# A second level of the seven-product form inside two of seven products, in an attention and MoE kernel that TensorE bounds

## The chip, the cores and the metric

One core of one Trainium2 chip. The metric is the device time of one execution in microseconds (us), as the median over executions of the same kernel; lower is better. TensorE (PE in the profile) multiplies; VectorE (DVE), ScalarE (ACT) and GpSimd (POOL) do the rest; SyncE (SP) only issues transfers here.

## The reference, cut to what matters

```python
# q, k, v: (8 batches, 8 heads, 576, 64) fp32; w_in (512, 2048); w_out (2048, 512); alpha (2048)
k_p = k.reshape(B, H, 72, 8, D).mean(axis=3)       # keys and values pooled by 8: 72 of them
v_p = v.reshape(B, H, 72, 8, D).mean(axis=3)
attn = softmax(q @ k_p.T / sqrt(D))                # (the sum gets + 1e-9)
x = (attn @ v_p) ...  -> (4608 tokens, 512)
h = x @ w_in                                       # the first MoE product
s = sin(alpha * h)
g = h + s * s / (alpha + 1e-9)
return g @ w_out                                   # the second MoE product
```

## The kernel before

The 4608 tokens are cut into nine **units** of 512. A unit computes the first MoE product in four **groups**; a group is a 2x2 block product by the seven-product form (seven products where the plain form has eight), each product being 2 x 2 matmuls of 128x128 by 256 columns. So a unit has 28 **slots**, seven to a group. Into these slots the kernel puts, by hand, the attention of the batch that the next unit needs: scores, exps, normalisations, "turns" (32x32 transposes on VectorE), "moves" (twelve transfers from SBUF to SBUF that finish the transposition), and at the end the products with the values, which make the next unit's x. Sums of x and of the weights are made on VectorE.

The kernel uses eight PSUM banks. Five belong to the groups, three to the attention:

```python
    def bank(self, shape, i=None):
        if i is None:
            i = self.turn = (self.turn + 1) % 5           # five banks, in turn
        return self.ps_m.tile(shape, F32, name=f"bank{i}")
...
                self.ps_a = pool(att, "ps_a", 3, space=PSUM)
```

In a group the products follow one another in the order 1, 5, 6, 2, 7, 3, 4. Products 6 and 7 accumulate onto a *copy* of an earlier result, which ScalarE makes from one bank into another; the work on a finished product is put into the slot after it:

```python
            def left0(G=G, Q=before):                 # after product 1
                G.b6 = bank()
                nc.scalar.copy(out=G.b6[:], in_=G.b1[:])
                if Q and not early(Q):
                    squares(Q)
            def left1(G=G, Q=before):                 # after product 5
                if Q:
                    self.finish(Q)
            def left2(G=G, Q=before):                 # after product 6
                ...
                G.b7 = bank()
                nc.scalar.copy(out=G.b7[:], in_=G.b6[:])
                G.p5 = self.tp.tile([P, JW, TH], F32, name="p5")
                nc.scalar.copy(out=G.p5[:], in_=G.b5[:])
            ...                                       # left3 to left6: sines, squares, adds
            self.left = [(left0, left1, left2, left3, left4, left5, left6)[k]]
            if k == 1:
                G.b5 = bank()
            p = (1, 5, 6, 2, 7, 3, 4)[k]
            product(p, getattr(G, {1: "b1", 5: "b5", 6: "b6", 2: "b1", 7: "b7", 3: "b6", 4: "b7"}[p]), k < 2)
```

The slots of the attention in units 1 to 6:

```python
            for i in range(5):
                at((1, 3, 4, 5, 6)[i], A.score, i)
                at(8 + (i + 1) // 2, A.exp, i)
                at(9 + (i + 1) // 2, A.norm, i)
                at((12, 12, 13, 14, 14)[i], A.turn, i)
            at(14, A.new_a)
            at(14, A.move, 0)
            at(15, A.move, 1)
            for hp in range(4):
                at((0, 1, 3, 4)[hp], self.load_kv, "v", b, hp)
                ...
                at(24, A.values, hp)
            at(24, A.values_rest)
            turn = 21                                 # turns of the next q but one: slots 21 to 24
```

## Time and profile before

| | before |
|---|---|
| median time | 958.75 us (958.41 to 959.10) |
| span of the profiled run | 956.4 us, mean granted clock 1.000 |
| busy: PE, DVE, ACT, POOL | 98%, 71%, 43%, 21% of the span |
| one unit of 2 to 6 | 57.20 us, no wait of TensorE in it |

The lines behind this stand in the prediction below. How to read them: the busy shares say only which engine to look at first; the chain of waits says what the end of the run hangs on; the table of stretches says whether a repeated part (here the unit) is one engine's work end to end. The last is the strongest here: a unit of 57.20 us that holds 57.20 us of TensorE work cannot be shortened by anything but less TensorE work, and is lengthened by any wait.

### The profile page before, as it was taken

To read this page: it belongs to the slowest core of one execution; us is meant where nothing else is said; L and a number is where in the kernel's file an instruction comes from. 1 tells how busy PE (TensorE), PEld (TensorE's weight loads), DVE (VectorE), ACT (ScalarE), POOL (GpSimd) and SP (SyncE) were. 2 spreads that over 40 slices of the span, in tenths; PEclk is the share of its full clock that TensorE was granted. 3 is DMA by queue.
4 is the path that set the end of the run, shared out by engine and by line. 5 is a ranking of instruction groups with operands and counts; after the bars stand their busy time and mean duration, and the time that the engine had idled before them with its cause. 6 is when DMAs were issued, how large, how long until landed. Compare 5 with 4: busy or idle time off the path is not lost.

```text
span 956.4 us, 18152 instructions
## 1 busy us (share of the span) xinstructions
PE 937.6 (98%) x7259; PEld 833.4 (87%) x7259; DVE 676.5 (71%) x1070; ACT 414.2 (43%) x919; POOL 197.7 (21%) x215
## 2 busy tenths in 40 slices
PE   7998999999999999999999999999999999999998
PEld 3677687887878878787888899999999999999998
DVE  5889585766838577483576996867768695958684
ACT  5376466575756747566555531111111111111111
POOL 1717364443724436260000000000000000000000
PEclk9999999999999999999999999999999999999999
DMA  9636466666576663745615235324142434343201
GB/s 222 176 104 198 125 195 142 205 149 196 171 198 201 156 190 102 188 136 161 242 54 206 98 142 190 125 102 161 67 155 78 143 115 147 98 139 122 100 34 35
DMA packets 84038, 137.88 MB, mean 144 GB/s; under 512 B 10177, under 2 KB 49873, under 8 KB 79345
## 3 DMA queue, kind: packets, MB, share of 16 engines
q1 hardware_dynamic: 83920, 136.70, 47.1%
q8 instruction: 58, 0.95, 0.4%
q14 instruction: 26, 0.21, 0.1%
q10 hardware_dynamic: 34, 0.02, 0.0%
HBM read 74.47 MB, written 47.19 MB: 127 GB/s over the span
## 4 chain that ended last, share of the span: by engine, by line
PE 92%; DVE 4%; ACT 2%; DMA 1%; issue 0%; SPq 0%; DVEq 0%; ACTq 0%
PE bank L489 42%; PE bank L752 30%; PE ps_y L752 12%; PE ps_o L309 3%; PE ps_sc L208 2%; DMA q<-in_q_dram 1%; DVE as L368 1%; ACT s L495 1%; PE ps_at L267 1%; DVE home L462 1%; DVE a L372 1%; PE ps_qt L189 1%; PE bank L452 1%; DVE h L468 0%; PE ps_or L318 0%
## 5 line engine op out<-in xcount | busy, mean ns | idle before, releaser
L489 PE MATMUL bank<-home,a 128*128 128x256 f32 x1152 | 266.3, 382 | 3.0 <-DVE h L468 1.6
L489 PEld LDWEIGHTS bank<-home,a 128*128 128x128 f32 x1152 | 215.3, 190 | 36.6 <-DVE h L468 3.1
L489 PE MATMUL bank<-home,as 128*128 128x256 f32 x864 | 201.6, 382 | 2.8 <-DVE as L368 1.6
L489 PEld LDWEIGHTS bank<-home,as 128*128 128x128 f32 x864 | 161.7, 190 | 26.7 <-ACT bank L507 2.4
L105 POOL TENSOR_TENSOR kvin<-kvin 72x512 f32<-72x512 f32 x112 | 126.0, 1125 | 180.3 <-DMA kvin<-in_v_dram 112.0
L495 ACT ACTIVATE s<-h,rat 128x256 f32<-128x256 f32 x144 | 65.2, 500 | 90.2 <-DVE h L468 90.2
L468 DVE TENSOR_TENSOR h<-bank,p 128x512 f32<-128x512 f32 x72 | 49.1, 682 | 74.7 <-ACT s L497 47.4
L752 PE MATMUL bank<-wb,home 128*128 128x128 f32 x712 | 92.1, 275 | 0.0
L752 PEld LDWEIGHTS bank<-wb,home 128*128 128x128 f32 x712 | 85.7, 192 | 0.0
L831 ACT COPY bank<-bank 128x128 f32<-128x128 f32 x63 | 15.8, 250 | 149.3 <-PE bank L752 149.2
L497 ACT ACTIVATE s<-s 128x512 f32<-128x512 f32 (+1 forms) x106 | 77.8, 768 | 1.1
L495 ACT ACTIVATE s<-bank,rat 128x256 f32<-128x256 f32 x144 | 59.9, 467 | 36.9 <-PE bank L489 24.4
L752 PE MATMUL bank<-wb,xe 128*128 128x128 f32 x512 | 67.6, 275 | 0.0
L752 PEld LDWEIGHTS bank<-wb,xe 128*128 128x128 f32 x512 | 62.4, 192 | 0.1
L844 ACT COPY bank<-bank 128x128 f32<-128x128 f32 x63 | 15.8, 250 | 96.6 <-PE bank L752 96.6
L250 POOL TENSOR_TENSOR ex<-ex,sm 128x576 f32<-128x576 f32 (+1 forms) x38 | 42.5, 1148 | 46.5 <-DVE sm L249 21.4
L549 DVE TENSOR_TENSOR h<-h,s 128x1024 f32<-128x1024 f32 x36 | 44.5, 1237 | 0.0
L549 DVE TENSOR_TENSOR h<-bank,s 128x512 f32<-128x512 f32 x36 | 24.5, 681 | 24.5 <-ACT s L497 23.9
L819 ACT COPY bank<-ps_y 128x256 f32<-128x256 f32 x63 | 22.5, 357 | 35.9 <-PE ps_y L752 35.9
L519 ACT COPY bank<-bank 128x512 f32<-128x512 f32 x36 | 20.6, 571 | 39.4 <-PE bank L489 39.4
L712 DVE TENSOR_TENSOR xe<-home 128x512 f32<-128x512 f32 x30 | 19.4, 687 | 25.5 <-PE bank L752 25.4
L215 DVE TENSOR_REDUCE mx<-ps_sc 128x4 f32<-128x288 f32 (+1 forms) x75 | 33.6, 448 | 4.4 <-PE ps_sc L208 4.4
(152 smaller groups left out, 1499.3 us busy)
## 6 DMA issues: line engine op xcount, KB each, us to landing
g_bridge<-h SPq DMA_DIRECT2D x36, 1024.0 KB
r<-g_bridge SPq DMA_DIRECT2D x18, 1024.0 KB
home<-g_bridge SPq DMA_DIRECT2D x18, 1024.0 KB
out_dram<-o SPq DMA_DIRECT2D x36, 256.0 KB
q<-in_q_dram SPq DMA_DIRECT2D x8, 1024.0 KB
kvin<-in_k_dram SPq DMA_DIRECT2D x28, 288.0 KB
kvin<-in_v_dram SPq DMA_DIRECT2D x28, 288.0 KB
a<-in_moe_w_in_dram SPq DMA_DIRECT2D x16, 256.0 KB
```

The lines of the kernel that those rows point to most:

```text
L105: (eng or nc.gpsimd).tensor_tensor(out=o, in0=t[:, :, 0:w], in1=t[:, :, w:2 * w], op=OP.add)
L215: nc.vector.tensor_reduce(out=mx[:n], in_=ps[:n], axis=AX, op=OP.max)
L250: eng.tensor_tensor(out=E(n, i, 0, H), in0=E(n, i, 0, H), in1=sm[:n].unsqueeze(2).to_broadcast([n, H, Sp]), op=OP.mult)
L309: nc.tensor.matmul(ps[64 * e:64 * e + 64, :], vp[:, h, :], x, start=True, stop=True)
L468: add = lambda o, x, y: nc.vector.tensor_tensor(out=o, in0=x, in1=y, op=OP.add)
L489: nc.tensor.matmul(ps[:, jj, :], self.A[p][:, kk, f * P:(f + 1) * P], x[:, kk, :], start=(start and jj == 0 and kk == 0), stop=(kk == 1), ...
L495: nc.scalar.activation(out=G.s[:, i, j, jj, :], in_=src[:, jj, :], func=AF.Sin, scale=self.rat[:, f:f + 1])
L497: square = lambda G, x: nc.scalar.activation(out=x, in_=x, func=AF.Square)
L519: nc.scalar.copy(out=G.b7[:], in_=G.b6[:])
L549: add = lambda o, x, y: nc.vector.tensor_tensor(out=o, in0=x, in1=y, op=OP.add)
L752: nc.tensor.matmul(out, A[:, J, :], W[:, J // 2, J % 2, :], start=(start and J == 0), stop=(J == self.NJ - 1), skip_group_check=True)
L819: nc.scalar.copy(out=x[:, 0:2, :], in_=yz[:, 0:1, :].to_broadcast([P, 2, P]))
```

## The change

Intent: products 1 and 5 of 17 groups (two in unit 1, three in each of units 2 to 6) are themselves 2x2 block products; do them in seven instead of eight pieces. The two products of a group, 16 instructions with 256 moving columns, become 28 with 128. The partial results are *grown in PSUM*: piece 1 and piece 5 go into a scratch bank, ScalarE seeds the product's bank from there, later pieces accumulate, VectorE copies and adds blocks in between, and all of it is spread over the slots of other products so that no hand-over should hold TensorE up.

To make room for these steps the change re-orders everything around them. The core of the diff:

```diff
+            def inner(G, p, q):
+                x, y = (G.b1, 0) if p == 1 else (G.b5, 2)
+                out = {1: self.y[:, y], 5: self.y[:, y + 1], 2: X(x, 0, 0), 3: X(x, 0, 1), ...}[q]
+                self.inner_product(p, G.J, q, out)
+                q5 = self.q5[:, y // 2]
+                if q == 6:
+                    nc.vector.tensor_copy(out=X(x, 1, 0), in_=X(x, 0, 1))
+                    add(X(x, 0, 1), X(x, 0, 1), q5)
+                elif q == 7:
+                    add(X(x, 1, 1), X(x, 1, 0), q5)
+            def seed(x, y):
+                nc.scalar.copy(out=x[:, 0]..., in_=self.y[:, y:y + 1].to_broadcast([P, 2, P]))
+                nc.scalar.copy(out=self.q5[:, y // 2], in_=self.y[:, y + 1])
+            if G.inner and k in (0, 2, 3):
+                for p, q in {0: ((1, 4), (5, 2), (5, 6)), 2: ((5, 3), (5, 7)), 3: ((5, 4),)}[k]:
+                    inner(G, p, q)
+            if soon and k in (3, 5, 6):
+                ...
+                for p, q in {3: ((1, 1), (1, 5)), 5: ((1, 2), (1, 6), (5, 1), (5, 5)), 6: ((1, 3), (1, 7))}[k]:
+                    inner(self.next, p, q)
```

The order of the products, and with it the place of the sines and squares (product 4 now runs behind the *next* group's product 1, product 5 stands fourth, not second):

```diff
-            p = (1, 5, 6, 2, 7, 3, 4)[k]
-            product(p, getattr(G, {...}[p]), k < 2)
+            if k == 0 and not G.inner:
+                self.product(G, 1, G.b1, True)
+            if k == 1 and J:
+                self.product(before, 4, before.b7)
+            if k == (3 if J else 1) and not G.inner:
+                G.b5 = self.bank([P, JW, TH], 2)
+                self.product(G, 5, G.b5, True)
+            if k == 2:
+                self.product(G, 6, G.b6)
+            ...                                       # k 4: 2, k 5: 7, k 6: 3 (and 4 of the last group)
```

Banks by number instead of in turn, one for the scratch y, and two for the attention from unit 1 on; and the attention's slots:

```diff
+    def begin_inner(self):
+        self.abanks = (6, 7)
+        self.y = self.bank([P, 4, P], 5)
...
-                at((1, 3, 4, 5, 6)[i], A.score, i)
-                at(8 + (i + 1) // 2, A.exp, i)
-                at(9 + (i + 1) // 2, A.norm, i)
-                at((12, 12, 13, 14, 14)[i], A.turn, i)
-            at(14, A.new_a)
-            at(14, A.move, 0)
-            at(15, A.move, 1)
+                at((1, 3, 5, 7, 9)[i], A.score, i)
+                at((9, 9, 10, 10, 11)[i], A.exp, i)
+                at((10, 10, 12, 14, 14)[i], A.norm, i)
+                at((14, 16, 16, 16, 17)[i], A.turn, i)
+            at(18, A.new_a)
+            at(18, A.move, 0)
+            at(18, A.move, 1)
...
-                at(24, A.values, hp)
+                at(25 + hp // 2, A.values, hp)
...
+                at(((3, 5, 6, 6) if u == 1 else (0, 2, 3, 3))[part], self.turn_q, u + 2, part)
```

Also changed, and cut here: weight sums for the pieces (made on VectorE in unit 1) and sums of x (GpSimd) for them; two of the four ordinary sums of x go to GpSimd; k is fetched before it is pooled; unit 0's weight sums, a_t and values move by a slot or more; the sums of the second weight in units 7 and 8 are cut into halves. And two buffers are shared to make room: the exps of a unit and the moved attention weights now lie in one buffer (`xa`), where the kernel before had two (`ex` and `aT`), so the next unit's scores can't be written before the values have read it.

## The prediction

> **What bounds the kernel now.** I read the page's busy shares first, then the chain of waits in order of time, then the table of stretches, then the list of who waited for whom. The busy row alone proves little, since matmul ends are modelled, but the chain that ended last says the same:
>
> ```profile
> PE 937.6 (98%) x7259; PEld 833.4 (87%) x7259; DVE 676.5 (71%) x1070; ACT 414.2 (43%) x919; POOL 197.7 (21%) x215
> PE 92%; DVE 4%; ACT 2%; DMA 1%; issue 0%; SPq 0%; DVEq 0%; ACTq 0%
> ```
>
> TensorE is 92% of the chain. The kernel has a start (0 to about 44 us), nine units of the first MoE product (unit 0 to about 104 us, units 1 to 6 of 57.2 us each, units 7 and 8 to about 557 us), then the second product to the end, which already uses two levels of the seven-product form. The stretches of units 2 to 4, cut at the first value product of each:
>
> ```profile
> core 0: us, PE busy (x) PEld busy (x) DVE busy (x) ACT busy (x) POOL busy (x), PEclk, DMA share, GB/s
> 161.35:218.55 57.20, 57.20 (x422) 46.79 (x424) 37.70 (x65) 36.70 (x72) 27.00 (x29) 1.00 0.66 180
> 218.55:275.75 57.20, 57.20 (x423) 46.79 (x424) 37.52 (x65) 36.70 (x72) 25.97 (x29) 1.00 0.67 180
> 275.75:332.95 57.20, 57.20 (x423) 46.79 (x424) 36.88 (x65) 36.70 (x72) 27.09 (x29) 1.00 0.66 178
> ```
>
> The unit repeats to the hundredth of a microsecond, at full clock, with DVE at 66%, ACT at 64% and POOL at 47%. Nothing but TensorE's own stream sets 57.20. The waits of TensorE over the whole run are short and all lie in the start and in unit 0:
>
> ```profile
> PE ps_al L339 <- DMA s<-in_moe_alpha_dram: 3.8, 1, 3.8
> PE ps_at L267 <- DVE aT L269: 2.0, 1, 2.0
> PE bank L489 <- DVE as L368: 1.6, 1, 1.6
> PE bank L489 <- DVE h L468: 1.6, 1, 1.6
> PE bank L489 <- ACT bank L519: 1.4, 1, 1.4
> PE ps_qt L189 <- DVE q L91: 1.3, 1, 1.3
> PE bank L489 <- ACT bank L507: 1.0, 1, 1.0
> PE ps_kt L177 <- ACT aT L269: 0.8, 1, 0.8
> ```
>
> From unit 1 on there is no wait at all: a gain there must come out of TensorE's work, and any new wait there is a loss in full. The price of the two sizes of matmul, from the chain in order of time:
>
> ```profile
> 244.43 31.32 PE bank L489 x144
> ...
> 566.83 4.47 PE bank L752 x40
> 573.09 4.47 PE bank L752 x40
> ```
>
> A fp32 matmul is two instructions here. With 256 moving columns (L489) one costs 31.32 / 144 = 217.5 ns. With 128 (L752) the two rows are one product of the second stage apart, that is 56 instructions (40 here, 16 into ps_y), so one costs (573.09 - 566.83) / 56 = 111.8 ns.
>
> **What the Trainium skill says.** "TensorE: Matmul & The Clock Gate", section LDWEIGHTS, gives a weight load as columns / 1.2, so 107 ns for 128 columns; that would leave nothing hidden under a 128-column matmul. The trace agrees that they nearly meet: 111.8 ns, and LDWEIGHTS at 25.00 of 25 us in several stretches of the second stage, yet the pace holds. "Perfetto Trace Analysis", section Identifying the Most-Contended Engine, says to judge TensorE by LDWEIGHTS share: 46.79 / 57.20 = 82% in a unit, which the change raises. "PSUM — Partial Sum Buffer", section on bank collisions, demands that two engines never touch one bank at a time; so each copy in PSUM that the change adds is a hand-over TensorE may have to wait for. "SBUF — State Buffer", section Who interferes with whom, has a VectorE instruction with two SBUF inputs and a GpSimd one block each other: in the trace two 72x512 adds of POOL take 2.07 us undisturbed and up to 3.25 beside DVE.
>
> **The change part by part.** The nested groups are those from 6 to 27 whose number is not a multiple of four: 2 in unit 1 and 3 in each of units 2 to 6, 17 in all.
>
> TensorE: products 1 and 5 of a group were 2 x 4 matmuls of 256 columns, 16 instructions x 217.5 = 3.48 us. They become 2 x 7 matmuls of 128 columns, 28 x 111.8 = 3.13 us. The gain is 0.35 us a group, 1.05 us a unit, **17 x 0.35 = 5.95 us**. At the border from L489 to L752 in unit 8 the trace shows no price for mixing sizes (8 small ones take 0.89 us there, the next 8 large ones 1.73). Score products do cost about 0.2 us at a border (8 large before a score take 1.92, not 1.74); their number stays. The values now stand in two slots rather than one: one border more in units 1 to 6, at about 0.15 us, **-0.9 us**.
>
> ACT gets for each nested product a spread copy of y (128x256 from PSUM into PSUM, 357 ns at L819) and a copy of 128x128 (250 ns at L831): 4 copies, 1.2 us a group, 3.6 a unit; 36.7 becomes 40.3 of about 56 us, 72%.
>
> DVE gets a copy and two adds of 128x128 per product. Reading 128x256 and 128x512 from PSUM takes 415 and 681 ns, so 128 columns are an estimated 280 ns: 6 x 0.28 x 3 = 5.0 us a unit; two 128x512 sums (0.69 each) leave for POOL: 37.4 becomes about 41, 73%. In unit 1 alone it also has eight weight sums (128x384, est. 0.55) and four of x, about 5.5 us.
>
> POOL gets those two sums (est. 1.05 to 1.15 from the 72x512 and 128x576 rows) and eight sums of 128x128 (0.5 from the 72x128 row): 6 us a unit.
>
> So no other engine becomes the bound on average. What changes is slack. Before, TensorE waited on ACT copies with a product or more (1.74 us) to spare. Now it needs, two or three times a group, a DVE copy-and-add within about 2.2 us of the small product, and product 6 needs the DVE add of the last group and the ACT copy behind it, chained in one slot. I worked out about 0.25 us to spare there.
>
> Two places look short. At the head of units 2 to 6, POOL must pool v0 (2.5 us), make two sums (2.1), pool v1 (2.5) and only then make the first nested sum, wanted some 6.2 us into the unit. v0 can be fetched early, since the DMAs that turn q no longer stand before it (they held it until 232.54); with the landing of 4 to 6 us that the trace shows I get the sum at 5.8 to 6.4 us, and the second product's sum 0 to 0.8 us late. And where the five exps and two table loads (1.28 us each) stand ahead of a seed on ACT, I get about 0.6 us late. Estimate: 0 to 1.2 us a unit, taken as 0.4 over units 2 to 6, and 1 us for the crowded unit 1: **-3 us**.
>
> Unit 0 keeps its products, but its weight sums, a_t and values move. The waits there (2.0 on aT, 1.6 on h, 1.0 and 1.4 on bank, 0.8 on k_t) come from DVE's and ACT's backlog; the weight sums now end at slot 17, before the a_t of slots 21 to 24. I take back 2.5 of these 6.8: **+2.5 us**. Units 7 and 8 and the second stage had no waits to lose; the finer pieces of the second weight's sums only protect that.
>
> Sum: 5.95 - 0.9 - 3 + 2.5 = 4.5 us; 958.75 - 4.5 = 954.2.
>
> **Rivals.** (a) Everything lands in time: 5.95 - 0.9 + 4 of unit 0 is about 9 us, 949.5. For it speaks that the moves (scores two slots apart with two banks, turn of q out of the crowded slots, sums to POOL) are those of someone who removes waits. (b) The hand-overs make a wait in each nested group. One DVE instruction of 0.7 to 1.2 us in the way each time would be 17 x 0.7 = 12 us lost, 965. DVE ran without a gap for ten microseconds at a unit's head, so this is possible there; against it, DVE idles in the later groups. (c) POOL or the DMA queue becomes the bound at the head of the units: v landing 4 us later costs 5 x 4 = 20 us, 974. (d) The attention, down to two PSUM banks, waits for its own evacuation: 1.8 us of DVE for a score against 3.5 us between scores, so little.
>
> **Range and chances.** The most that the matmuls can give is 0.6% of the time, so 2% faster (939.6) is out of reach unless TensorE's pace changes; 2% slower (977.9) needs a wait of over 1.5 us in all 17 groups or (c) in full. I say **954.2 us, 948.5 to 962**; faster 0.01, same 0.94, slower 0.05.
>
> **What would show it.** Units 2 to 6 at 56.0 to 56.8 us; TensorE's list of waits with POOL, DVE or ACT entries of under 1 us at the head of a unit if I am right, and in every nested group if (b) is; TensorE instructions up by 17 x 12 = 204; small matmuls still 111.8 ns apart; the second stage unmoved. The prediction would be wrong most easily through POOL's queue behind v, or if small matmuls beside large ones are paced differently than in the second stage.

## The result, and the profile after

| | before | after |
|---|---|---|
| median time | 958.75 us | 1016.69 us (1012.84 and 1020.55) |
| ratio to before | | 1.0604 (1.0431 to 1.0778) |
| span of the profiled run, clock | 956.4 us, 1.000 | 1018.8 us, 0.979 |
| TensorE instructions | 7259 | 7463 |

A ratio in this document is the mean time of one kernel's fast runs over that of the other's in the same rounds, so it is not quite the quotient of the medians. The change is **slower by 6%**, outside the range of the prediction. Of the profiled span's 62.4 us, the time to the first value product of unit 1 (161.28 to 180.59) gives 19.3, units 2 to 6 give 40.7, and the rest 2.4.

The page of the changed kernel: busy shares, the clock row and the shares of the chain.

```profile
PE 964.7 (95%) x7463; PEld 850.5 (83%) x7463; DVE 714.4 (70%) x1184; ACT 431.5 (42%) x987; POOL 245.3 (24%) x280
...
PEclk9999999899998999989999999999999999999999
...
PE 64%; DVE 11%; ACT 7%; POOL 6%; DMA 4%; SPq 4%; issue 2%; DVEq 0%; ACTq 0%; POOLq 0%
```

No other engine is near its limit: DVE's share is lower than before. Yet the chain has gone from 92% TensorE to 64%, and passes through DVE, ACT, POOL and the transfers. And the clock row has slices of 8, which the kernel before has not. Both say: not more work, but a stream that stops.

The table of stretches, cut at the first value product of each unit (columns as in the prediction):

```profile
core 0: us, PE busy (x) PEld busy (x) DVE busy (x) ACT busy (x) POOL busy (x), PEclk, DMA share, GB/s
180.59:246.52 65.93, 61.94 (x456) 49.40 (x457) 42.79 (x80) 39.14 (x84) 33.28 (x40) 0.95 0.55 154
246.52:310.21 63.69, 58.88 (x456) 48.02 (x457) 43.37 (x80) 39.60 (x85) 33.04 (x40) 1.00 0.58 164
310.21:376.73 66.52, 62.07 (x457) 49.30 (x457) 42.80 (x80) 40.20 (x86) 33.61 (x40) 0.95 0.56 157
376.73:440.36 63.63, 58.88 (x456) 48.02 (x457) 42.80 (x80) 39.54 (x85) 33.51 (x40) 1.00 0.51 143
```

Two things are to be seen. A unit at full clock takes 63.66 where 57.20 - 1.05 = 56.15 was to come out; of the 7.5 us between, 4.8 are idle (63.69 - 58.88) and 2.7 are *busy time beyond the work* (58.88 - 56.15). A part of this is how a stop is drawn: a matmul of 256 columns lasts 385 ns in the trace, but in the stream the next one starts after 217.5, so at each of the unit's eight listed waits some 0.17 us more count as busy (an estimate of 1.3 us in all). The mix of sizes is not the cause: where a small matmul follows a large one it starts after 216 ns, and where a large one follows a small one, after 112 (medians of the unit from 246.52). The rest of the 2.7 us is not explained here. And every second unit is 2.2 to 2.9 us longer at a granted clock of 0.95.

Who TensorE waited for, over the whole run (total, times, longest):

```profile
PE bank L331 <- DMA xa<-tr: 12.4, 6, 2.9
PE bank L534 <- ACT bank L611: 7.0, 9, 4.3
PE bank L521 <- POOL inr L494: 4.8, 5, 2.7
PE bank L534 <- ACT bank L594: 4.7, 11, 0.8
...
PE bank L521 <- DVE bank L545: 3.8, 10, 0.6
...
PE bank L534 <- POOL home L489: 2.0, 1, 2.0
```

L331 is the value product: six waits of about 2 us for the moves, one in each of units 1 to 6. L611 and L594 are the ACT copies into the banks of products 7 and 6. L521 is a small piece, waiting for its sums (POOL, L494) or for DVE's copy-and-add (L545). The list as shown is cut; with the lines left out it comes to some 50 us.

Where the clock falls can be seen in the order of time. One unit with the half clock, then the next without (start, duration, instruction; in brackets the idle time before and what ended it):

```profile
310.21 2.76 PE L331 MATMUL bank<-xa,vp 72*64 72x512 f32 x8 [1.63 <-DMA xa<-tr]
312.90 3.78 PE L534 MATMUL bank<-home,a 128*128 128x256 f32 x8
...
376.73 1.94 PE L331 MATMUL bank<-xa,vp 72*64 72x512 f32 x8 [2.10 <-DMA xa<-tr]
378.60 1.99 PE L534 MATMUL bank<-home,a 128*128 128x256 f32 x8
```

The same eight large matmuls take 3.78 us or 1.99. The stretch at half clock follows the wait for the moves, but not every time, and not for the longer of these two waits. The clock's own record shows why. In this run every half-clock stretch starts on one grid of steps of 3.413 us (those at 181.49, 311.20, 440.90 and 509.17 us lie 38, 38 and 20 steps apart) and lasts one or two steps, 3.41 or 6.83 us (the one at the program's end is cut short). So it counts how a wait falls into a step:

```profile
307.79:311.20 3.41, 1.78 (x11) 1.05 (x11) 0.69 (x1) 2.56 (x5) 0.00 (x0) 1.00 0.77 217
311.20:318.03 6.83, 6.83 (x18) 3.12 (x16) 1.23 (x1) 2.73 (x8) 2.77 (x3) 0.50 0.87 303
372.64:376.05 3.41, 1.99 (x10) 1.59 (x9) 0.69 (x1) 2.56 (x7) 0.00 (x0) 1.00 0.67 134
```

The wait of 1.63 us lies whole in one step: TensorE is busy for 1.78 of its 3.41 us, and the next two steps are at half clock. The wait of 2.10 us is cut in two by a step's end at 376.05: 1.99 us are busy before it, 2.73 of 3.41 after it, and the clock stays. Two units together last 130.15 us, 38.1 steps, which fits that the half clock comes back in every second unit. How much idle time in a step is enough, the runs don't say sharply: half clock followed a step with 2.16 us busy (no_nested, from 480.38) and did not follow one with 1.45 (turns_early, from 97.63).

### The profile page after: what moved, and what is told of

It reads as the page before. It is cut to its first block, busy times and chain, and to the rows that moved or that the text cites.

```text
span 1018.8 us, 18814 instructions
## 1 busy us (share of the span) xinstructions
PE 964.7 (95%) x7463; PEld 850.5 (83%) x7463; DVE 714.4 (70%) x1184; ACT 431.5 (42%) x987; POOL 245.3 (24%) x280
## 4 chain that ended last, share of the span: by engine, by line
PE 64%; DVE 11%; ACT 7%; POOL 6%; DMA 4%; SPq 4%; issue 2%; DVEq 0%; ACTq 0%; POOLq 0%
PE bank L885 39%; PE bank L534 18%; POOL kvin L114 3%; PE bank L331 2%; DMA xa<-tr 2%; SPq L307 2%; DVE home L489 2%; SPq L161 2%; ACT s L653 2%; ACT xa L234 2%; PE bank L217 1%; POOL xa L259 1%; DMA q<-in_q_dram 1%; DVE h L545 1%; DVE tr L298 1%
## 5 line engine op out<-in xcount | busy, mean ns | idle before, releaser
L534 PE MATMUL bank<-home,a 128*128 128x256 f32 x1016 | 253.0, 398 | 9.0 <-ACT bank L611 7.0
L534 PEld LDWEIGHTS bank<-home,a 128*128 128x128 f32 x1016 | 194.2, 197 | 47.3 <-issue 8.9
L534 PE MATMUL bank<-home,as 128*128 128x256 f32 x728 | 174.0, 386 | 4.7 <-ACT bank L594 4.7
L534 PEld LDWEIGHTS bank<-home,as 128*128 128x128 f32 x728 | 134.7, 191 | 24.9 <-ACT bank L594 7.0
L885 PE MATMUL bank<-wb,home 128*128 128x128 f32 x928 | 118.2, 275 | 0.0
L885 PEld LDWEIGHTS bank<-wb,home 128*128 128x128 f32 x928 | 110.8, 192 | 0.0
L545 DVE TENSOR_TENSOR h<-bank,p 128x512 f32<-128x512 f32 x72 | 49.2, 683 | 63.2 <-PE bank L534 63.0
L259 POOL TENSOR_TENSOR xa<-xa,sm 128x576 f32<-128x576 f32 (+1 forms) x38 | 44.0, 1174 | 86.2 <-DVE sm L258 71.1
L885 PEld LDWEIGHTS bank<-wb,xe 128*128 128x128 f32 x512 | 62.4, 192 | 0.1
L594 ACT COPY bank<-bank 128x512 f32<-128x512 f32 x36 | 20.5, 570 | 69.5 <-PE bank L534 37.4
L224 DVE TENSOR_REDUCE mx<-bank 128x4 f32<-128x288 f32 (+1 forms) x75 | 33.5, 447 | 12.5 <-PE bank L217 12.1
L331 PE MATMUL bank<-xa,vp 72*64 72x512 f32 x96 | 27.7, 702 | 12.4 <-DMA xa<-tr 12.4
L885 PE MATMUL bank<-a,xe 128*128 128x128 f32 x288 | 38.0, 275 | 0.0
```

The lines of the kernel that those rows point to most:

```text
L224: nc.vector.tensor_reduce(out=mx[:n], in_=ps[:n], axis=AX, op=OP.max)
L259: eng.tensor_tensor(out=E(n, i, 0, H), in0=E(n, i, 0, H), in1=sm[:n].unsqueeze(2).to_broadcast([n, H, Sp]), op=OP.mult)
L331: nc.tensor.matmul(ps[64 * e:64 * e + 64, :], vp[:, h, :], x, start=True, stop=True)
L534: self.nc.tensor.matmul(ps[:, jj, :], self.A[p][:, kk, f * P:(f + 1) * P], x[:, kk, :], start=(start and jj == 0 and kk == 0), stop=(kk == ...
L545: add = lambda o, x, y: nc.vector.tensor_tensor(out=o, in0=x, in1=y, op=OP.add)
L885: nc.tensor.matmul(out, A[:, J, :], W[:, J // 2, J % 2, :], start=(start and J == 0), stop=(J == self.NJ - 1), skip_group_check=True)
```

## The experiments

Eighteen kernels ran, in six batches. The kernel before ran beside them each time, at medians between 957.82 and 959.66 us. Every kernel but one (said there) gave the right result. The slot numbers in the short diffs are those of units 1 to 6 unless told otherwise.

**Taking the nested products out of the changed kernel.** All else stays.

```diff
-                self.inner = {n for n in range(self.NJ + 2, (self.B - 1) * self.NJ) if n % self.NJ}
+                self.inner = set()          # and no sums for the pieces
```

> The changed kernel with all of its new order and places, but no nested products: the set of nested groups is empty and their sums are left out. Theory A (late turns and moves of the attention weights): TensorE gets 1.9 us more of work between the moves and the values, so the wait of the values on xa<-tr shrinks from about 2.1 us a unit to 0 to 0.7, the half-clock stretches of units 1, 3 and 5 go, units about 58 to 60 us, time 970 to 985. Theory B (the hand-overs of the nested groups cost the time): waits on bank and inr in units 2 to 6 vanish, but the waits on xa<-tr stay at about 2 us and the half clock with them, time 985 to 995. If the new order itself (product 4 moved behind, one buffer for s) is to blame, the time stays over 995.

Measured: 996.3 us, ratio 1.0385 (1.0361 to 1.0409), clock 0.992: over 995, the case that the expectation laid to the new order itself. So the nested products with their sums, in these slots, cost 20 us (a rough size, since the two runs of the changed kernel lie 7.7 us apart), and the reorganisation without them 37.

**Turns and moves three slots earlier**, with the nested products and without.

```diff
-                at((10, 10, 12, 14, 14)[i], A.norm, i)
-                at((14, 16, 16, 16, 17)[i], A.turn, i)
-            at(18, ...)                     # new_a, move 0, move 1
+                at((10, 10, 11, 11, 12)[i], A.norm, i)
+                at((12, 13, 13, 14, 14)[i], A.turn, i)
+            at(15, ...)
```

> The changed kernel with nested products, but norm, turn and move of the attention weights three slots earlier (turns done by slot 14, moves at slot 15). Theory A: the moves end about 5 us earlier, the 12.4 us of waits on xa<-tr go to nearly 0, the half-clock stretches behind them go (about 10 us), 1016 becomes 985 to 995 and the mean clock over 0.99; units 2 to 6 at about 60.5 us, even ones like odd ones. Theory B: the moves were only late because TensorE was slowed; the time is made up elsewhere and stays within 5 us of 1016, or the DVE work that comes earlier makes the nested hand-overs slower by as much.

> Both edits: no nested products and the earlier turns. Theory A: units 2 to 6 back at 57.2 to 57.6 us without a wait, only units 0 and 1 longer than in the kernel before, 962 to 972. Theory B: the same as without nested products alone within 3 us. The difference between this run and the one with earlier turns and nested products is the price of the nested products with the moves out of the way: theory B needs it to be over 15 us, I expect 15 to 25 with the 4 us of hand-over waits a unit.

Measured: 1004.2 us (1.0478; 1.0448 to 1.0507) with nested products, 1011.3 us (1.0566; 1.0526 to 1.0606) without. With them, 12.5 us of the loss go (less than theory A's 985 to 995 asked for); without them, it gets *worse* by 15. Both theories for plain_turns (962 to 972, or within 3 us of no_nested) failed. Its longest waits are on VectorE's adds of h (14.2 us in six). My reading of the trace: v is fetched after sixteen small transfers that turn q, these take 10.8 us of SP's time to issue, v is pooled late, the divisions wait behind it, and VectorE waits for them. In the changed kernel these issues look like this (SP's own queue):

```profile
332.24 10.82 SPq L161 DMA_DIRECT2D q<-tr  x16
343.16 0.50 SPq L104 DMA_DIRECT2D kvin<-in_v_dram  x1
```

**The late slots alone, in the kernel before.** Only norm, turn and move as in the changed kernel.

```diff
-                at(9 + (i + 1) // 2, A.norm, i)
-                at((12, 12, 13, 14, 14)[i], A.turn, i)
-            at(14, ...); at(14, ...); at(15, ...)
+                at((10, 10, 12, 14, 14)[i], A.norm, i)
+                at((14, 16, 16, 16, 17)[i], A.turn, i)
+            at(18, ...)
```

> The kernel before with nothing changed but the slots of norm, turn and move, set to those of the changed kernel. Theory A: the turns end about 4 us later, the moves of 10 us no longer fit in front of the values, 1 to 2 us of wait in each of six units and in some of them a half-clock stretch that costs about 3 us more: 968 to 980, mean clock below 1.000. Theory B: the moves still fit, or the wait is too short to matter: 958 to 962.

Measured: 1016.4 us, ratio 1.0601 (1.0569 to 1.0634), clock 0.968. Both expectations were far too low. By itself this one move of slots costs as much as the whole change. Its largest wait, from the list of who waited for whom, is less than half of its loss:

```profile
PE ps_o L309 <- DMA aT<-tr: 20.4, 6, 3.8
```

The order of time of the same run shows what comes after one of these waits:

```profile
236.08 7.09 PE L309 MATMUL ps_o<-aT,vp 72*64 72x512 f32 x16 [3.19 <-DMA aT<-tr]
```

In the kernel before, the same sixteen value matmuls take 3.65 us. In all, the half clock took 32.4 us in this run, summed as one minus the granted clock over its microseconds (the last stretch, at the program's end, left out); in the changed kernel the same sum is 20.5, in the kernel before 0. (The changed kernel has its values one slot later, and longer units, so the same late moves make a smaller wait there: 12.4 us.)

**Is it really the clock?** On top of before_late, dummy matmuls (identity by identity, into a bank that nobody reads) ahead of the values keep TensorE running where it would wait.

```diff
+                if hp == 0:
+                    at(24, self.warm)      # 14 matmuls of 128 columns, about 3.1 us
                 at(24, A.values, hp)
```

> The kernel before with the late turns and moves, and 14 dummy matmuls of 128 columns (28 instructions, about 3.1 us) into a spare bank ahead of the values of units 1 to 6, where TensorE otherwise waits 3.4 us. They take no longer than the wait. If the half clock behind the waits is a cost of its own, the mean clock returns to about 1.000 (from 0.968) and about 30 us come back: 980 to 990. If the clock is no effect of the wait, or the dummies only delay the values, 1012 to 1030.

Measured: 982.6 us, ratio 1.026 (1.0244 to 1.0276), clock 0.998. The moves stand in the same slots as in before_late, TensorE does *more* work, and 34 us are gone. So in before_late about 34 of 57 us were the half clock after the waits, and 23 the waits and the rest.

The same in the changed kernel, ten dummy matmuls ahead of the values of units 1 to 6 (about 2.2 us):

> The changed kernel with 10 dummy 128-column matmuls (20 instructions, about 2.2 us) ahead of the first value product of units 1 to 6, so that TensorE does not stand still while it waits for the moves. If half-clock stretches behind that wait are a large part of the loss (20.5 us of lost clock in the profiled run of the changed kernel, most behind the value waits of alternate units), it should run at 1000 to 1006 us with a mean clock of 0.990 or more, and the units with a stretch should shorten from 66.5 to about 64. Rival: the half clock starts at other, nested hand-overs as well; then 1010 to 1016.

Measured: 1006.7 us, ratio 1.0492 (1.0474 to 1.0509), clock 0.993: a hair above the expected 1000 to 1006. No unit from 2 on is longer than 64.6 us now, and the alternation is gone:

```profile
304.60 2.40 PE L478 MATMUL bank<-ident 128*128 128x128 f32 x20
307.14 1.94 PE L331 MATMUL bank<-xa,vp 72*64 72x512 f32 x8
```

So the half clock behind the value waits is worth about 10 us of the 58 (the two runs of the changed kernel alone lie 7.7 us apart, so the size is rough), and the wait itself, filled here, is still paid.

**Fetching v ahead of the q turns.** On top of the early turns, without and with nested products, and then with one more thing: the left-over add of the group before ahead of the nested copy-and-add.

```diff
-                at((0, 1, 3, 4)[hp], self.load_kv, "v", b, hp)
+                at((0, 0, 0, 1)[hp], self.fetch_kv, "v", b, hp)
+                at((0, 0, 3, 5)[hp], self.pool_kv, "v", b, hp)
```
```diff
+            if G.inner and k == 0:          # nest_v_left only
+                for f in self.left:
+                    f()
+                self.left = []
```

> No nested products, earlier turns, and all four v fetches of a unit issued in slots 0 and 1, so ahead of the 16 DMAs that turn q (they stood behind v3's turn in slot 3 for 10.8 us); v2 and v3 are pooled in slots 3 and 5. Theory C (the turn of q in front of v3 on the DMA queue keeps POOL from dividing the exps, and DVE and ACT wait behind it): the 5.3 us wait on h and the half clock after it go, units 2 to 6 at 57.2 to 58.5 us, time 962 to 972. Theory D (the new order of products with one buffer for s is the cause, whatever the DMA queue does): waits on bank and h stay at 3 to 5 us a unit, time over 990.

> The same edits with the nested products kept. Theory C: waits on xa<-tr gone, waits of the nested groups down to about 2 us a unit (copy-and-add hand-overs), units 2 to 6 at 58 to 60 us, unit 1 still about 70, time 978 to 990. If the hand-overs of nested groups cost what the earlier pair suggests (theory B), units stay at 62 or more and the time over 995.

> As the run before, and the add of the last group (which product 6 waits for through the ACT copy of b6) put ahead of the nested copy-and-add on DVE in the first slot of a nested group. The waits on the b6 copy (0.5 and 0.3 us in two of three groups) should go: 2 to 5 us less than the run before. If DVE's order is not the cause, no difference over 1 us.

Measured: 1004.3 us (1.0467; 1.0449 to 1.0486), 1000.7 us (1.0443; 1.0417 to 1.0468) and 996.2 us (1.0387; 1.0369 to 1.0406). The theory that v's place was the cause expected 962 to 972 for plain_v and 978 to 990 for nest_v, and failed: early v brought 7 us without nested products, and 3.5 with them, where the intervals of the ratios overlap. In these slots the nested products no longer lose: 1011.3 against 1004.2 with early turns, 1004.3 against 1000.7 with v early (intervals that overlap). That is 4 to 7 us, around the predicted 5.95 of saved matmuls, but the pairs differ in their waits too, so it isn't a measurement of the 5.95; and with the late turns the same products cost 20 us. The best kernel with them so far (996.2) is no faster than no_nested (996.3). What remains of waits from 235.8 to 483.1 us, four units, in nest_v_left:

```profile
PE bank L521 <- DVE bank L545: 10.2, 12, 1.4
PE bank L521 <- POOL inr L494: 2.9, 4, 0.8
...
```

Twelve waits of 0.85 us on DVE's copy-and-add, in four units of three nested groups: one in each nested group. That is the prediction's rival (b), and nearly its size (0.7).

**All these mends, and the crowded units 0 and 1 relieved**: nested groups only from unit 2 on (weight sums late in unit 1), q's pairs a slot later and norms spread in unit 0.

```diff
+            at(19, self.inner_sums, 1, (1, 2, 3))   # in unit 1; they stood at 6 and 10
+            at(22, self.inner_sums, 5, (1, 2, 3))
```

> All of these, nested products in units 2 to 6 only (15 groups), the weight sums late in unit 1, and in unit 0 the q copies behind the b7 copy and two norms behind the add that frees s. Units 0 and 1 lose about 12 us of waits and half clock: 955 to 968. It beats the kernel before only if the hand-overs of a nested unit cost less than the 1.05 us that the small matmuls save; I expect 0 to 10 us over it.

Measured: 994.3 us, ratio 1.0367 (1.0348 to 1.0387), far from the expected 955 to 968. Two us better than nest_v_left, with intervals that just overlap: this mend didn't take. The first value product of unit 1 comes at 175.0 us here, at 174.3 in nest_v_left and at 161.3 in the kernel before, so units 0 and 1 still lose some 13 us; among their waits is one of 5.5 us on GpSimd's sum of x. The other 23 lie in units 2 to 6 (61.8 us each).

**Nested products with the attention slots of the kernel before.** The turns of q go back to slots 21 to 24 too, v is pooled later (slots 5 to 8), and the left-over add and the mends of units 0 to 2 stay.

```diff
-  scores (1, 3, 5, 7, 9), exps (9, 9, 10, 10, 11), norms (10, 10, 12, 14, 14), turns (14, 16, 16, 16, 17), moves 18
+  scores (1, 3, 4, 5, 6), exps (8, 9, 9, 10, 10), norms (9, 10, 10, 11, 11), turns (12, 12, 13, 14, 14), moves 14, 15
```

> Nested products in units 2 to 6, with the attention's exps, norms, turns, moves and turn of q back in the slots of the kernel before, v pooled behind the sums on POOL, and the fixes of units 0 and 1. If the crowding of the middle of the unit by late exps and turns is what is left of the loss, units 2 to 6 come to 57 to 58.5 us and the time to 958 to 970, less than the best nested one so far (994). If the new order and the hand-overs cost it wherever the attention stands, 980 to 1000.

Measured: 1048.0 us, ratio 1.0934 (1.09 to 1.0967), the worst of all and outside both expectations (958 to 970, 980 to 1000), clock 0.969, with 21.3 us of waits on the ACT seeds alone. The later slots are not a slip: with nested products the old ones are worse.

**The order of products alone.** The kernel before with the new order and what it forces (product 4 behind the next group's product 1, product 5 fourth except in a unit's first group, sines and squares following, banks by number, and the first two sums of x moved from the end of a unit to the head of the next).

> The kernel before with one thing of the change: the new order of products in a group (product 4 goes behind product 1 of the next group, the sines and squares of the group follow it, the first two sums of a unit move into its slot 0 because the old ones are still in use at slot 26). Attention slots, banks, turn of q and POOL work are those of before. Theory E (the new order takes the slack: after product 3 only 2 products, 3.5 us, pass until product 6 needs the bank again, where 3 products, 5.2 us, passed before): waits on bank and h of 1 to 4 us in each unit and some half clock, 970 to 990. Theory A alone (late turns and moves): no wait after unit 0, 956 to 962.

Measured: 1031.6 us, ratio 1.0768 (1.0742 to 1.0794), above both expectations. Its **result was wrong** (relative error 0.19): a sum of the second weight in slot 20 of unit 8 wrote over a weight slice that product 3 now reads later. Mended below by one slot; the table loads seen here (1.28 us each; the unit from 241.38 has four, between exps and the moved sines, where a unit of the kernel before has two) are mended with it:

```diff
-  slots of the second weight's sums in unit 8: (6, 10, 13, 14, 17, 20); exps 8 + (i + 1) // 2
+                                               (6, 10, 13, 14, 17, 21); exps (9, 9, 10, 10, 11), norms (10, 10, 11, 11, 12)
```

> The kernel before with the new order of products only, and right this time (the last sums of the second weight one slot later; the exps gathered in slots 9 to 11 as in the changed kernel, so that the sine and exp tables are not changed back and forth). The run with old exp slots took 1031.6. If its 25.8 + 9.9 us of waits on ACT came from table loads between the exps and the moved sines, it should fall to 970 to 985. Rival: the new order itself has too little slack on the banks (product 6 and 7 two products behind the last reader, not three), and it stays above 1000.

Measured, with a right result: 1006.6 us, ratio 1.0503 (1.0473 to 1.0532). The two mends are worth 25 us, but the theory expected 970 to 985 and the rival, "stays above 1000", holds. **The new order with what it forces, without one nested product, costs 48 us**: 11 of them before the first value product of unit 1, 23 in units 2 to 6, and 13 after. A unit of it:

```profile
233.96:296.19 62.23, 58.30 (x420) 47.25 (x421) 39.84 (x65) 37.18 (x72) 27.89 (x29) 1.00 0.61 165
```

420 instructions, as many as before within the gaps of the record; but 3.9 us idle, and 58.30 us busy where the kernel before had 57.20. Its waits over four units, from 233.9 to 481.6 us:

```profile
PE bank L476 <- DVE h L487: 4.7, 4, 1.2
PE ps_sc L208 <- issue: 4.0, 4, 1.0
PE bank L476 <- ACT bank L536: 2.9, 4, 0.7
PE bank L476 <- ACT bank L553: 2.4, 4, 0.6
```

One of each of these four in each unit: an add of h (DVE) before its bank is used again, and the copies into the banks of products 6 and 7. Counted in the code, three products (4, 1 and 5, 5.2 us) stood in the old order between product 3, which an add on VectorE must read out, and the next group's product 6, which follows that add; in the new order two (1 and 4, 3.5 us). That this lost slack is the cause is argued from the waits; no run changes it alone. (The second line is laid to nothing by the profile. In the unit shown the wait ends at 255.01, just after VectorE has read a score out of its bank, at 254.91; with the scores spread these waits are gone.)

**Scores spread, and finer weight sums, in that order.**

```diff
-                at((1, 3, 4, 5, 6)[i], A.score, i)
+                at((1, 3, 5, 7, 9)[i], A.score, i)
```

> The right version of the kernel before with the new order of products, plus one thing: the scores at slots 1, 3, 5, 7, 9 as in the changed kernel instead of 1, 3, 4, 5, 6. In the new order alone a unit of 1 to 6 takes 61.8 us, of which 3.8 are waits: on DVE adds of h that stand behind score work, and on the ACT copies into the two banks. If the loss is DVE's queue behind the scores, units fall to 59 or less and the time to 985 to 992. Rival: the two-product slack on the banks and the moved sines make the waits wherever the scores are; then 61 to 62 a unit and 1000 to 1006.

> The same, and the sums of the second weight in units 7 and 8 in the finer pieces and the slots of the changed kernel. In the new order alone the part after the last value product took 522.4 us against 509.1 before and 512.2 in the changed kernel without nested products, with three ACT waits of 6.9 us in all and a half-clock stretch. If the finer pieces are what mends it: 8 to 11 us faster than the run without them. Rival: worth under 3 us, and the rest of units 7 and 8 comes from elsewhere.

Measured: 993.9 us (1.0365; 1.0343 to 1.0387) with units of 59.9, between what the two theories expected; so VectorE's queue behind bunched scores was part of it (12.7 us); the slack on the banks, as the other part, is not tested. With the second weight's sums in the finer pieces of the changed kernel as well: 982.1 us (1.0253; 1.0236 to 1.0271), another 11.8 us, where 8 to 11 were expected; the three ACT waits of 6.6 us in units 7 and 8 are gone.

**What lies between this and the 996.3 of the changed kernel without nested products?** Two banks for the attention, or the late turns and moves:

```diff
-                self.ps_a = pool(att, "ps_a", 3, space=PSUM)
+                self.ps_a = pool(att, "ps_a", 2, space=PSUM)
```

> The new order of products with spread scores and finer weight sums (982.1), and the attention held to two PSUM banks instead of three, as in the changed kernel. My prediction's rival (d) called this a small matter. If it is: 980 to 986, units of 60.0. Rival: the two banks are what lies between 982 and the 996 of the changed kernel without nested products; then 990 to 1000, with waits of the score and value products on DVE and ACT.

> The same with three banks, and with the normalisations, turns and moves of the attention in the changed kernel's slots (norms 10, 10, 12, 14, 14, turns 14, 16, 16, 16, 17, moves 18), the values still in slot 24. In the kernel before these slots alone cost 57 us, 20.4 of it waits on the move and some 34 half clock. If a unit that is 2.8 us longer lets the moves land nearer in time, the wait shrinks to 1 to 2.5 us a unit: 995 to 1015. Rival: in this order late turns relieve VectorE and cost nothing: 978 to 985.

Measured: two banks 998.1 us (1.0407; 1.0382 to 1.0432). That looks like the rival's size, but the place is wrong: the first value product of unit 0 comes at 123.75 instead of 108.64, and units 2 to 6 take 60.3 each instead of 60.0. The loss is in unit 0, where the changed kernel has three attention banks. In the units concerned, two banks cost some 0.3 us a unit. The late slots cost 50 us here (1032.4 us, outside the expected 995 to 1015; 1.0769, 1.0734 to 1.0803; clock 0.966), with values in slot 24: seven waits of 29.1 us in all on the ACT copy into product 7's bank, and 8.8 us on the moves. So neither tells where the 14 us lie: the changed kernel without nested products needs 62.0 us a unit (171.66 to 481.65 over five) against 60.0, of which 4.1 us in all are waits for the moves. The rest is **left open**. Not separated by any run: the buffer that exps and moved weights now share, the turn of q at the head of the unit, sums of x on GpSimd, and the values a slot later.

**Unit 0 alone.** The kernel before with the weight sums of unit 0 at the changed kernel's slots.

```diff
-                at((4, 10, 14)[J - 1], self.combine_w_in, J, 0)
-                at((6, 12, 20)[J - 1], self.combine_w_in, J, 1)
+                at((4, 9, 15)[J - 1], self.combine_w_in, J, 0)
+                at((6, 11, 17)[J - 1], self.combine_w_in, J, 1)
```

> The kernel before with the weight sums of unit 0 at slots 4, 9, 15 and 6, 11, 17 as in the changed kernel, nothing else. My prediction took 2.5 us back in unit 0 from this and from the moved a_t. If it is worth anything alone: 955 to 958. Rival: the sums only move the wait elsewhere in unit 0: 958 to 961.

Measured: 960.8 us, ratio 1.0018 (1.0008 to 1.0028). No gain: a slight loss. No kernel of these experiments beats the kernel before.

The main runs in one table; a unit is the mean of units 2 to 6 (five intervals from first value product of unit 1 to that of unit 6).

| kernel | nested | median us | a unit, us | clock |
|---|---|---|---|---|
| before | no | 958.8 | 57.2 | 1.000 |
| new order, scores spread, finer sums (rotated_sp_w) | no | 982.1 | 60.0 | 0.993 |
| new order, scores spread (rotated_sp) | no | 993.9 | 59.9 | 0.990 |
| new order alone (rotated_ok) | no | 1006.6 | 61.8 | 0.989 |
| changed, without nested (no_nested) | no | 996.3 | 62.0 | 0.992 |
| changed, mended (nest_v_left) | yes | 996.2 | 61.8 | 0.995 |
| changed, dummies before values (after_warm) | yes | 1006.7 | 63.9 | 0.993 |
| changed (after) | yes | 1016.7 | 65.3 | 0.979 |

## Why the prediction was wrong, point by point

**The matmuls (+5.95 us): right as far as seen.** 204 instructions came as counted (7463 - 7259). Small matmuls still go at 111.8 ns in the second stage: the rows at 640.90 and 649.84 of the trace there are 80 instructions apart, 8.94 / 80. With early turns the two pairs with and without nested products differ by 4 to 7 us in their favour, which fits 5.95 but doesn't isolate it. "No price for mixing sizes" held.

**The other engines' load: right, and beside the point.** DVE was predicted at about 41 us a unit and measured at 42.8, ACT at 40.3 and measured at 39.5. No engine became the bound on average. Where other engines made TensorE wait, it was by when they came to an instruction, not by how much they had to do. Two small misreadings decide nothing: the "two 72x512 adds" of 2.07 us are one of 512 columns and one of 256 (undisturbed 1.27 and 0.73 us), and the 1.92 us of eight matmuls before a score run to the last one's end, so they are no pace to set against 1.74.

**The failed step is the term "-3 us" for waits.** It priced only two hand-overs, at the head of the units and behind the exps. Measured, waits and what follows them cost about 60 (57.9 us lost in place of 4.5 won, so 62 off the sum). What the term left out:

1. *The new order of products was not priced at all.* I read it as a re-labelling that leaves the same work. rotated_ok: 48 us by itself; 24 with spread scores and finer sums (rotated_sp_w), two parts of the change that I had not counted as needed. A stream with no wait has slack that no view lists; the reorder seems to have spent it: two products in place of three between product 3 and product 6 (counted in the code, not tested alone).
2. *The waits for the moves were not foreseen.* I counted the value products' extra border (0.9 us) but did not follow the chain scores, exps, norms, turns, moves to its new end. The exps end a slot later, the turns three, and the moves start four slots later. In the changed kernel the wait is 12.4 us, and the moves' early slots win 12.5 (turns_early), with the half clock in it.
3. *The half clock was not foreseen.* A wait of 2 us can be followed by several us in which TensorE runs at half its pace: 10 us in the changed kernel (after_warm), 34 in before_late (late_warm). So a wait may cost more than twice its length (57 us in before_late, for 20.4 of listed waits); my sum priced each at its length.
4. *The nested hand-overs.* I gave 0 to 1.2 us a unit. nest_v_left shows 0.85 us in each nested group on DVE, and restarts on top: rival (b), which I thought possible but less likely. In the changed kernel itself the same waits are short (3.8 us over 10); that longer waits elsewhere hide them is my reading.

The parts don't add up in a simple sum, and they aren't meant to: the same late turns cost 57 us in the old order, 50 in the new with spread scores, and 15 us *less than the early ones* in no_nested against plain_turns.

**Unit 0 (+2.5 us): wrong.** before_u0 shows no gain from the weight sums (1.0018); the moved a_t and values were not run alone. In the changed kernel, unit 0 and the head of unit 1 lost 19 us: a copy into product 7's bank that stood on ACT behind a score that came late from VectorE (ACT idle for 6.45 us until 47.15) and behind copies of q (4.3 us), an a_t (3.7) and three waits of 1.5 to 2.7 in unit 1. I had looked at which of the old waits would go and not at what the moved work would meet.

**Rivals.** (a) did not come. (b) was true in nature once other waits were gone. (c) was true in kind, v behind sixteen transfers of q, but small: 1004.2 to 1000.7, within the noise. (d), two attention banks, was rightly called small: 0.3 us a unit (sp_w_two).

**The range.** A range of 948.5 to 962 took the profile's silence on waits for slack. With a stream of zero waits and the order of a whole group changed, the upside was bounded at 0.6% by the matmuls and the downside by nothing that I had measured. Slower by over 2% should have had far more than 5%. ("(c) in full" comes to 974 in the prediction's own sum, so it would not have reached 977.9.)

## What to carry to other kernels

When an engine's stream has no wait, work out how much slack each hand-over has (time from the last reader of a buffer to its next writer, against the queue of the engine between) *before* re-ordering it; the saved work is an upper bound, the lost slack is not. Test the reorganisation without the idea that it serves: no_nested shows 37 of the 58 us without one nested product, and rotated_ok 48. And price a wait of TensorE with its aftermath, restart and possibly half clock, by filling it with dummy matmuls, as late_warm and after_warm do.

## What the Trainium skill lacked or had wrong

- "TensorE: Matmul & The Clock Gate", Part 1 (the clock gate), has the clock fall to one half after an idle window of about 3.4 us. Here a window needn't be idle: the clock fell after a wait of 1.63 us that left TensorE busy for 1.78 of the 3.41 us of its step (310.21), and not after one of 2.10 us that a step's end cut in two (376.73). On the window's 3413 ns, and on its running free of the kernel, the traces agree with the page: all half-clock stretches of a run lie on one grid of that step. Its second failure mode, short idling between groups of matmuls, did not show: 19 waits in four units of rotated_ok (233.9 to 481.6 us) have no half clock among them. The price of the half clock here is about 10 us of 58 (after_warm) and 34 of 57 (late_warm).
- No page says what a stop in a stream of matmuls costs beyond the wait's own length. Here a unit of the same 420 instructions is busy for 58.30 us instead of 57.20 when 19 waits in four units interrupt it (rotated_ok): an estimate of at most 0.23 us for each wait (1.10 / 4.75), of which 0.17 are the last matmul's time to its modelled end.
- "DMA: Bandwidth & Descriptors", section Issuing engines are not separate DMA queues, calls the time to start a DMA usually small relative to the DMA itself. For small transfers it adds up on the sequencer: sixteen small transfers took 10.82 us to issue here, 0.68 us each, and v waited behind them. How long one of them takes to land, no run here shows.
- No page says how to see slack in a stream without waits. It was the missing number here: a view of waits is empty in units 1 to 6 of the kernel before, and 48 us came from the order of its products and what that forced.
